# Attention with a soft-capped score, then a soft mixture of experts: a second set of VectorE work buffers and a new table of places

## The chip, the cores and the metric

The kernel runs on one core of one Trainium2 chip, as one program. The metric is the device time of one execution in microseconds (us). The core has a matrix engine (TensorE, PE in the profile; its weight loads are PEld), VectorE (DVE), ScalarE (ACT), GpSimd (POOL) and an engine that here only issues transfers (SyncE, SP). Each engine works through its own instructions in the order in which they were written, and waits on semaphores for the others.

## The reference

```python
# 8 batches, 12 heads, 448 positions, head size 64; cap = 30
scores = cap * np.tanh(scale * (q @ k.T) / cap)
attn   = np.exp(scores - scores.max(-1))             # divided by its sum over the row
x      = (attn / attn.sum(-1)) @ v                   # -> 3584 tokens x 768
logits = x @ phi                                     # 32 slots: 8 experts x 4
d      = softmax(logits, axis=0)                     # over all tokens
slot_input = d.T @ x                                 # 32 x 768
slot_out[e] = np.maximum(slot_input[e] @ w1[e], 0) @ w2[e]   # 768 -> 1024 -> 768
out    = softmax(logits, axis=1) @ slot_out          # 3584 x 768
```

So there is a long attention part, whose output is needed whole before the experts can run (the softmax over all tokens), and a short tail: two small matrix layers with large weights, and an output of 11 MB.

## The kernel before, in words

**Tiles, chunks, steps.** A quad is four heads of a batch, a pair two of them; a pair's scores are 7 tiles of 128 x 448, in each of them 64 keys of either head against its 448 queries. All 336 tiles stand in one list, and six of them are a chunk; there are 56 chunks, and the main loop (L893) has one step j for each. In step j PE makes scores of the next chunk (`qk_chunk`), ACT takes the tanh of chunk j out of PSUM (`tanh_chunk`, L366, two instructions of three tiles, 128x1344) and the exponential of chunk j-1 in SBUF (`exp_chunk`, L374), and PE multiplies the exponentials of a finished pair with v (`pv_first`, `pv_rest`, L627). DVE divides by the row sum (`norm`, L634 and L637).

**Joined tanhs.** For chunks in the tuple `JOINED` the tanh is one instruction over all six tiles (L362, 128x2688). From the first to the last of them the scores have one buffer of six banks, the board, whose halves are written and read in turn; after a joined tanh the scores of the next chunk can begin only when it has ended.

**Shared chunks.** ACT doesn't take all exponentials. In the chunks of the table `SHARED`, DVE computes those of the first one, two or three tiles itself, by seven instructions on the bits of the numbers (`poly_exp`, L596 to L611): four on a tile and constants (tensor_scalar: L602, L604, L606, L609) and three on two tiles (tensor_tensor: L605, L607, L608). They work in place in `ex` and in two work buffers, `xf` and `xp`; the second entry in `SHARED` numbers the set of work buffers, and before there is one set. The exponential of ACT in such a chunk is shorter by those tiles. The table `POLY` says where each of the seven is written: at step j and slot (`'0'`, `'m'`, `'e'`, `'a'` to `'d'`, with `<` and `>` for before and after the other work of a slot).

**Other work in the steps.** `WHEN` says where the rest stands: loads of q and k (on POOL's queue, L185), their transposes by PE with a copy by DVE (`transp`, L281), the transposes of x (`x_transp`, L689), and after each batch its logits, their exponentials E (`e_exp`), the sums over tokens (`slot_sums`, L778), the transposed E (`e_transp`, L733) and their sums (`e_sums`, L743). Before, the table is the same for every batch, shifted by 7 steps. `FILL` and a few single lines write matrix multiplications of ones (`fill`, L657, into unused columns of the pv bank; `spare`, L876) whose results nobody reads.

**The tail** (from L930) ends the last pairs, sums, and runs the two layers (`layer1` L1070, `layer2` L1098). The first layer's weights and part of the second layer's are in SBUF by then; of the second layer's 32 parts (`w2_parts`, 384 KB each) the first `KEPT` are held in SBUF as `w2b`, and the others were cast into DRAM (`w2d`) and are fetched by SP into memory that the attention gives back (`w2t`, L1049). Then 28 output tiles of 128 tokens are multiplied, scaled by ACT and DVE in turn (L1140, L1142 for half tiles, L1193, L1195), and stored by SP (L1126). The last two batches' E are transposed there, between output tiles, by `e_transp`, and their sums are formed by `e_recips` (L748, L751).

The order on every engine is the order in which the program is written (`manual_schedule`); nothing moves an instruction afterwards.

Of the kernel before, what the change touches and what calls it, by code (L numbers as in the profile page):

```python
# [37 lines left out]
def kernel(  # L38
# [28 lines left out]
    KEPT = 11  # L67
# [19 lines left out]
    ET4 = consts.tile([P, B // 2 - 1, NT, 2, HP], BF16, name="ET4")  # L87
# [7 lines left out]
    consts.tile([P, 336], BF16, name="pad")  # L95
# [46 lines left out]
    xf = [wk.tile([P, 3 * S], U16, name="xf")]  # L142
    xp = [wk.tile([P, 3 * S], F16, name="xp")]
# [232 lines left out]
    def exp_chunk(j):  # L376
# [4 lines left out]
    JOINED = (10, 14, 17, 21, 24, 28, 29, 31, 35, 38, 42, 45, 49)  # L381
    SHARED = {1: (2, 0), 3: (3, 0), 4: (3, 0), 6: (2, 0), 7: (3, 0), 9: (3, 0), 11: (3, 0), 12: (3, 0), 14: (3, 0), 16: (3, 0), 18: (3, 0), 19: (3, 0), 21: (3, 0), 23: (3, 0), 25: (3, 0), 26: (3, 0), 28: (3, 0), 30: (3, 0), 32: (3, 0), 33: (3, 0), 35: (3, 0), 37: (3, 0), 39: (3, 0), 40: (3, 0), 42: (3, 0), 44: (3, 0), 46: (3, 0), 47: (2, 0), 48: (2, 0), 49: (3, 0), 51: (2, 0), 52: (1, 0), 53: (3, 0), 54: (1, 0)}
    POLY = {(1, 'm'): ((1, 0),),
            (1, 'e'): ((1, 1),),
            (1, '>a'): ((1, 2),),
            (1, '>b'): ((1, 3),),
            (1, '>d'): ((1, 4),),
            (2, 'r'): ((1, 5),),
            (3, 'e'): ((3, 0),),
            (3, '<a'): ((3, 1), (1, 6)),  # L390
            (3, '<b'): ((3, 2),),
            (3, '>c'): ((3, 3),),
            (4, '<a'): ((3, 4),),
            (4, '>a'): ((3, 5),),
            (4, '<c'): ((4, 0),),
            (5, 'e'): ((4, 1), (3, 6)),
            (5, '<a'): ((4, 2),),
            (5, '>b'): ((4, 3),),
            (5, '>c'): ((4, 4),),
            (6, 'e'): ((6, 0), (4, 5), (6, 1)),  # L400
            (6, '<a'): ((4, 6),),
            (6, '>d'): ((6, 2),),
            (7, 'm'): ((6, 3),),
            (7, 'e'): ((7, 0),),
            (7, '>a'): ((6, 4),),
            (7, '<b'): ((6, 5),),
            (7, '<d'): ((7, 1),),
            (8, '0'): ((7, 2), (7, 3)),
            (8, '>b'): ((6, 6), (7, 4)),
            (8, '>c'): ((7, 5),),  # L410
            (9, 'm'): ((9, 0),),
            (9, '<a'): ((7, 6),),
            (9, '>b'): ((9, 1),),
            (9, '>d'): ((9, 2),),
            (10, 'e'): ((9, 3),),
            (10, '>b'): ((9, 4),),
            (10, '>d'): ((9, 5),),
            (11, 'e'): ((11, 0),),
            (11, '<a'): ((9, 6),),
            (11, '>a'): ((11, 1),),  # L420
            (11, '>b'): ((11, 2),),
            (11, '<c'): ((11, 3),),
            (11, '>c'): ((11, 4),),
            (12, '<a'): ((12, 0),),
            (12, '<b'): ((11, 5),),
            (12, '<c'): ((12, 1),),
            (12, '>d'): ((11, 6),),
            (13, '<b'): ((12, 2),),
            (13, '>b'): ((12, 3),),
            (13, '>c'): ((12, 4),),  # L430
            (13, '>d'): ((12, 5),),
            (14, '<a'): ((14, 0), (12, 6), (14, 1)),
            (14, '<d'): ((14, 2), (14, 3)),
            (15, '>a'): ((14, 4),),
            (15, '>d'): ((14, 5),),
            (16, 'm'): ((14, 6),),
            (16, 'e'): ((16, 0),),
            (16, '<b'): ((16, 1),),
            (16, '>d'): ((16, 2),),
            (17, 'm'): ((16, 3),),  # L440
            (17, '<a'): ((16, 4),),
# [415 lines left out]
    for n in range(2):  # L857
        at(0, "c", vcast, 0, n)
# [376 lines left out]
```

## Time and profile before

| | |
|---|---|
| time, median of 3 runs | 281.52 us (280.67 to 281.65) |
| span of the profiled execution, first to last instruction | 279.2 us |
| busy: ACT, PE, DVE, POOL | 248.6, 247.0, 239.1, 142.0 us |
| granted TensorE clock, mean | 0.985 |
| tanh of three tiles (L366, 128x1344) | 85 times, 1.418 us |
| joined tanh (L362) | 13 times, 2.586 us |
| exponentials on ACT (L374) | 58 times, 110.7 us in all |
| output and weight traffic by SP | 32.02 MB |

The time is taken from outside, around the whole execution; the span lies inside of it, and the difference is what starts and ends a program. The busy time of an engine counts a moment once, also where one instruction begins before the one ahead of it has ended. In the view of groups, "x" is the number of instructions and the number behind the comma the mean duration of one in ns; in the view of time, the first column is the start and the second the duration in us, and what stands in brackets is the idle time of the engine before it and the engine that ended it.

### The profile page before, as it was taken

Reading aid. Unit: us, or ns where it says so; the run is one execution under the profiler, and the core shown is the slowest. Engines: PE = TensorE matmul, PEld = TensorE weight load, DVE = VectorE, ACT = ScalarE, POOL = GpSimd, SP = SyncE. Lnnn points to the kernel's source line nnn. Section 1 sums busy time; section 2 is a strip of 40 time slices with the busy share of each in tenths; the row PEclk is TensorE's granted clock in tenths of the full one; section 3 lists DMA queues with packets and bytes.
Section 4 is the critical chain, followed back from the end, with each engine's and each line's share of the span. In section 5 each row is a group of like instructions: output and inputs, shape, how many; then the busy total and the mean of one; then the engine's idle time right before and its main releaser. Section 6 shows DMA issues by size and latency. Waiting matters only on the chain.

```text
span 279.2 us, 10421 instructions
## 1 busy us (share of the span) xinstructions
PE 247.0 (88%) x4560; PEld 166.6 (60%) x4560; DVE 239.1 (86%) x473; ACT 248.6 (89%) x195; POOL 142.0 (51%) x198
## 2 busy tenths in 40 slices
PE   8898989998999999989999999899999999998720
PEld 7555556756675766566756675657566678553300
DVE  3479999999999999999999999999999997347940
ACT  4999999999999999999999999999999998237720
POOL 8796548662957296728673758375743230200000
PEclk9999999999999999999999999999999999999995
DMA  6999999999999999999999999999999588979997
GB/s 197 277 193 202 219 219 234 229 221 219 224 225 220 219 229 226 225 217 229 223 226 212 213 219 231 218 210 215 231 217 215 117 279 293 367 290 383 434 424 312
DMA packets 57340, 68.08 MB, mean 244 GB/s; under 512 B 4048, under 2 KB 53840, under 8 KB 56784
## 3 DMA queue, kind: packets, MB, share of 16 engines
q0 software_dynamic: 42448, 35.31, 80.0%
q1 hardware_dynamic: 14704, 32.02, 32.6%
q8 instruction: 35, 0.57, 0.7%
q10 hardware_dynamic: 144, 0.10, 0.1%
q14 instruction: 9, 0.07, 0.1%
HBM read 91.72 MB, written 19.27 MB: 398 GB/s over the span
## 4 chain that ended last, share of the span: by engine, by line
ACT 38%; DVE 27%; PE 27%; issue 3%; POOL 1%; ACTq 0%; DVEq 0%
ACT ex L366 15%; ACT ex L374 15%; PE pv L627 8%; ACT ex L362 6%; DVE xq L637 4%; PE sc L349 3%; DVE xp L605 3%; DVE xp L607 3%; DVE ex L608 2%; DVE ex L602 2%; PE so_ps L1098 2%; PE hp L1070 2%; DVE xf L604 2%; DVE ex L609 2%; DVE xp L606 2%
## 5 line engine op out<-in xcount | busy, mean ns | idle before, releaser
L366 ACT ACTIVATE ex<-sc 128x1344 f16<-128x1344 f32 (+1 forms) x87 | 112.9, 1402 | 0.9 <-PE sc L349 0.9
L374 ACT ACTIVATE ex<-ex 128x1344 bf16<-128x1344 f16 (+5 forms) x58 | 110.7, 1916 | 0.1
L627 PE MATMUL pv<-vbd,ex 128*128 128x130 bf16 (+1 forms) x1610 | 94.0, 212 | 7.6 <-POOL vbd L289 3.4
L627 PEld LDWEIGHTS <-ex 128*128 128x128 bf16 (+1 forms) x1680 | 75.6, 101 | 34.9 <-issue 6.2
L289 POOL CAST vbd<-vraw 64x896 bf16<-64x896 f32 x46 | 47.3, 1028 | 57.3 <-PE pv L627 35.7
L349 PE MATMUL sc<-qT,kT 64*64 64x448 bf16 x672 | 66.0, 359 | 6.7 <-ACT ex L366 4.8
L362 ACT ACTIVATE ex<-sc 128x2688 f16<-128x2688 f32 x13 | 33.6, 2586 | 0.0
L349 PEld LDWEIGHTS <-kT 64*64 64x64 bf16 x672 | 22.1, 105 | 16.3 <-ACT ex L366 6.9
L637 DVE TENSOR_TENSOR xq<-pv,rec 128x448 bf16<-128x448 f32 x46 | 28.7, 625 | 1.6
L607 DVE TENSOR_TENSOR xp<-xp,xf 128x1344 f16<-128x1344 f16 (+2 forms) x34 | 27.1, 798 | 0.6
L608 DVE TENSOR_TENSOR ex<-ex,xp 128x1344 uint16<-128x1344 uint16 (+2 forms) x34 | 26.9, 791 | 0.2
L605 DVE TENSOR_TENSOR xp<-xf 128x1344 f16<-128x1344 uint16 (+2 forms) x34 | 26.8, 789 | 0.2
L116 POOL DMA_DIRECT2D w1b<-in_moe_w_dram x32 | 26.3, 825 | 0.0
L602 DVE TENSOR_SCALAR ex<-ex 128x1344 uint16<-128x1344 f16 (+2 forms) x34 | 17.0, 500 | 1.4 <-ACT ex L366 0.8
L606 DVE TENSOR_SCALAR xp<-xp 128x1344 f16<-128x1344 f16 (+2 forms) x34 | 17.2, 505 | 0.6
L281 DVE COPY kT<-kps 128x896 bf16<-128x896 bf16 x23 | 14.2, 617 | 4.0 <-PE kps L276 2.8
L297 POOL MEMSET vbd<- 64x1 bf16 x22 | 2.8, 129 | 28.6 <-PE pv L627 28.3
L604 DVE TENSOR_SCALAR xf<-ex 128x1344 uint16<-128x1344 uint16 (+2 forms) x34 | 16.7, 491 | 0.4
L185 POOL DMA_DIRECT2D qb<-in_q_dram x22 | 16.3, 740 | 1.2 <-PE qps L279 0.5
L609 DVE TENSOR_SCALAR ex<-ex 128x1344 uint16<-128x1344 uint16 (+2 forms) x34 | 16.4, 483 | 0.4
L120 POOL DMA_DIRECT2D w2d<-in_moe_w_dram x21 | 16.4, 816 | 0.0
L185 POOL DMA_DIRECT2D kb<-in_k_dram x22 | 16.3, 739 | 0.0
(124 smaller groups left out, 320.2 us busy)
## 6 DMA issues: line engine op xcount, KB each, us to landing
w1b<-in_moe_w_dram POOLq DMA_DIRECT2D x32, 384.0 KB, 10.2
vraw<-in_v_dram SPq DMA_DIRECT2D x44, 224.0 KB, 6.2
w2d<-in_moe_w_dram POOLq DMA_DIRECT2D x21, 384.0 KB, 9.9
w2t<-w2d SPq DMA_DIRECT2D x21, 384.0 KB, 6.2
qb<-in_q_dram POOLq DMA_DIRECT2D x22, 224.0 KB, 8.2
kb<-in_k_dram POOLq DMA_DIRECT2D x22, 224.0 KB, 8.1
w2b<-in_moe_w_dram POOLq DMA_DIRECT2D x11, 384.0 KB, 9.5
out_dram<-ob SPq DMA_DIRECT2D x2, 1536.0 KB, 7.7
```

Of the source, the lines that this page charges most:

```text
L116: pool.dma_start(out=w1b[e][:, js, fs], in_=w1r[:, e, js, fs])
L185: pool.dma_start(out=t, in_=quad_ap(nm, Q))
L289: pool.tensor_copy(vbds[Q % 2][r, :, :, c0:c0 + DH], raw[r])
L349: ins = pe.matmul(sc[cs, u, 0:S], qkT["k", Q][r, c, cs], qkT["q", Q][r, :, cs], start=True, stop=True).ins
L362: apart["t", i - 1] = apart["t", i] = act.activation(exs[j].bitcast(F16), own["board"][:, :, 0:S], ACT.Tanh, scale=qk_scale / cap).ins
L366: ins = act.activation(exs[j][:, half * CS + u0:half * CS + u1, :].bitcast(F16), (own[0] if i == u0 == 0 else sc)[:, u0:u1, 0:S], ACT.Tanh ...
L374: act.activation(exs[j][:, u0:u1, :], exs[j][:, u0:u1, :].bitcast(F16), ACT.Exp, scale=cap)
L605: lambda: dve.tensor_tensor(p, s, s.bitcast(F16), op=ALU.mult),
L607: lambda: dve.tensor_tensor(p, p, s, op=ALU.mult),
L608: lambda: dve.tensor_tensor(y, y, p, op=ALU.add),
L627: pe.matmul(out_, exs[j][r, u, q0:q0 + (HP if tail else P)], v_, start=(c == 0 and g == gs[0] < NF), stop=(c == NT - 1), skip_group_check= ...
L637: dve.tensor_tensor(xq[Q][:, h, s0:s1, :], pv[:, 0:s1 - s0, 0:DH], rec.to_broadcast([P, s1 - s0, DH]), op=ALU.mult)
```

## The change

- `xf` and `xp` have two copies each (2 x 5.25 KB in each partition), and `SHARED` says for each chunk which set it uses. `SHARED` has 44 chunks for 34: 18 with three tiles, 15 with two and 11 with one, 95 tiles in all; before 27, 5 and 2, 93 tiles. With the new places in `POLY`, the seven instructions of two chunks can stand between one another.
- `JOINED` has 18 chunks for 13, from 7 to 53 for 10 to 49; four times two of them are neighbours (7 and 8, 22 and 23, 35 and 36, 52 and 53), before once (28 and 29).
- `WHEN` is written out for every batch and quad; `FILLS` lists eleven places with `fill` or `spare`; `fill` multiplications go from 262 to 33.
- The E of batches 4 and 5 are kept in buffers of their own and transposed in the tail with those of 6 and 7: `e_recips` and `e_transp` of batch 4 stand ahead of output tile 11, of batch 5 ahead of tile 12, and `e_transp` of the last two ahead of tiles 15 and 17 (before: 13 and 15). `ET4` holds two pairs of batches for three, `ETl` two for one.
- `KEPT` is 10 for 11: one part more of the second layer's weights goes by DRAM (22 for 21).

```diff
-    KEPT = 11
+    EARLY = 4
+    KEPT = 10
...
-    ET4 = consts.tile([P, B // 2 - 1, NT, 2, HP], BF16, name="ET4")
+    ET4 = consts.tile([P, EARLY // 2, NT, 2, HP], BF16, name="ET4")
...
-    xf = [wk.tile([P, 3 * S], U16, name="xf")]
-    xp = [wk.tile([P, 3 * S], F16, name="xp")]
+    xf = [wk.tile([P, 3 * S], U16, name=f"xf{n}") for n in range(2)]
+    xp = [wk.tile([P, 3 * S], F16, name=f"xp{n}") for n in range(2)]
...
-    JOINED = (10, 14, 17, 21, 24, 28, 29, 31, 35, 38, 42, 45, 49)
+    JOINED = (7, 8, 15, 17, 22, 23, 26, 31, 33, 35, 36, 38, 42, 45, 47, 49, 52, 53)
...
-            (55, '0'): ((54, 2),),
-            (55, 'e'): ((54, 3),),
-            (55, '<a'): ((54, 4),),
-            (55, '>a'): ((54, 5), (54, 6))}
+            (55, 'm'): ((53, 5),),
+            (55, 'e'): ((54, 3), (53, 6), (54, 4), (54, 5)),
+            (55, '>a'): ((54, 6),)}
...
     def e_exp(b):
-        es[b] = consts.tile([P, NG, NS], BF16, name="E", tag="E", bufs=2)
+        es[b] = consts.tile([P, NG, NS], BF16, name="E", tag="E", bufs=2) if b < EARLY or b >= B - 2 \
+            else consts.tile([P, NG, NS], BF16, name=f"E{b}")
...
+    def et_home(bb):
+        return ET4[:, bb] if bb < EARLY // 2 else ETl[:, bb - EARLY // 2]
...
-    FILL = ((7, 'a', fill, 25), (6, 'c', spare, 3), (5, 'a', fill, 10), (6, 'd', spare, 6),)
+    FILLS = ((15, '0', spare, 19), (7, '0', spare, 3), (12, 'd', spare, 3), (37, '0', spare, 9), (44, '0', spare, 7), (54, 'd', spare, 34), (33, 'b', fill, 3), (49, 'a', fill, 23), (7, '0', spare, 1), (35, 'a', fill, 7), (46, '0', spare, 1),)
...
-        if n == NH + 3:
-            e_transp(B - 1)
-        if n == NH + 5:
-            e_transp(B - 2)
+        for b, at_n in ((EARLY, NH + 1), (EARLY + 1, NH + 2), (B - 1, NH + 5), (B - 2, NH + 7)):
+            if n == at_n:
+                if b < B - 2:
+                    e_recips(b)
+                e_transp(b)
```

The end of the main loop on DVE, before: the rows from the last batch's sum of slots to the `norm` of the pair that ends in chunk 53. `ex_5289` is chunk 53's buffer (three tiles), `ex_5394` chunk 54's (one tile), `xT` is a copy of transposed x.

```order
L634 RECIPROCAL rec_5456<-pv_5399 128x7
L637 TENSOR_TENSOR xq_5398<-pv_5399,rec_5456 128x448
L689 COPY xT_5461<-xps_5462 128x896
L609 TENSOR_SCALAR ex_5289<-ex_5289 128x1344
L605 TENSOR_TENSOR xp_155<-xf_154 128x448
L606 TENSOR_SCALAR xp_155<-xp_155 128x448
L607 TENSOR_TENSOR xp_155<-xp_155,xf_154 128x448
L689 COPY xT_5504<-xps_5505 128x448
L608 TENSOR_TENSOR ex_5394<-ex_5394,xp_155 128x448
L609 TENSOR_SCALAR ex_5394<-ex_5394 128x448
L634 RECIPROCAL rec_5537<-pv_5490 128x7
L637 TENSOR_TENSOR xq_5398<-pv_5490,rec_5537 128x448
```

The same place on DVE now: between the same two `norm`s. `ex_5066` is chunk 53's buffer (three tiles, set 0), `ex_5171` chunk 54's (two tiles, set 1).

```order
L687 TENSOR_TENSOR xq_5176<-pv_5177,rec_5236 128x448
L657 TENSOR_TENSOR xp0_157<-xp0_157,xf0_155 128x1344
L655 TENSOR_TENSOR xp1_158<-xf1_156 128x896
L658 TENSOR_TENSOR ex_5066<-ex_5066,xp0_157 128x1344
L656 TENSOR_SCALAR xp1_158<-xp1_158 128x896
L659 TENSOR_SCALAR ex_5066<-ex_5066 128x1344
L657 TENSOR_TENSOR xp1_158<-xp1_158,xf1_156 128x896
L658 TENSOR_TENSOR ex_5171<-ex_5171,xp1_158 128x896
L739 COPY xT_5287<-xps_5288 128x448
L659 TENSOR_SCALAR ex_5171<-ex_5171 128x896
L684 RECIPROCAL rec_5319<-pv_5274 128x7
L687 TENSOR_TENSOR xq_5176<-pv_5274,rec_5319 128x448
```

Eight instructions of the polynomials stand between the two `norm`s, three of them over three tiles and five over two; before it was six, one over three tiles and five over one. Chunk 53, on which the next product with v waits, now ends in the middle of this piece.

The output tiles on DVE, before, from tile 11 on. `op` is a product in PSUM, `ob` the buffer for the stores, `eps` transposed E in PSUM.

```order
L1193 TENSOR_SCALAR ob_6179<-op_6181,winv_79 128x768
L733 COPY ETl_5797<-eps_6191 128x7x64
L1193 TENSOR_SCALAR ob_6189<-op_6197,winv_79 128x768
L733 COPY ETl_5797<-eps_6207 128x7x64
L1193 TENSOR_SCALAR ob_6205<-op_6213,winv_79 128x768
L1193 TENSOR_SCALAR ob_6205<-op_6221,winv_79 128x768
```

And now, for the same tiles:

```order
L802 TENSOR_REDUCE zdiag_86<-E4_3776 128x4
L805 RECIPROCAL winv_79<-zdiag_86 64x4
L805 RECIPROCAL winv_79<-zdiag_86 64x3
L787 COPY ETl_5581<-eps_5968 128x7x64
L1260 TENSOR_SCALAR ob_5963<-op_5986,winv_79 128x768
L802 TENSOR_REDUCE zdiag_86<-E5_4417 128x4
L805 RECIPROCAL winv_79<-zdiag_86 64x4
L805 RECIPROCAL winv_79<-zdiag_86 64x3
L787 COPY ETl_5581<-eps_5994 128x7x64
L1260 TENSOR_SCALAR ob_6015<-op_6017,winv_79 128x768
L787 COPY ETl_5581<-eps_6027 128x7x64
L1260 TENSOR_SCALAR ob_6025<-op_6033,winv_79 128x768
```

Eight instructions have come in ahead of tiles 11 and 13, and the copies that stood ahead of 13 and 15 stand ahead of 15 and 17.

More of the change, by code (lines that the diff above doesn't have):

```diff
@@ new lines @@
+            (21, '>b'): ((21, 1),),
+            (22, 'm'): ((21, 2),),
+            (22, 'e'): ((21, 3),),
+            (22, '<b'): ((21, 4),),
+            (22, '>b'): ((21, 5),),
+            (22, '<c'): ((22, 0),),
+            (22, '<d'): ((21, 6),),
+            (23, '0'): ((22, 1),),
+            (23, '>a'): ((22, 2),),
+            (23, '<b'): ((22, 3),),
+            (23, 'r'): ((22, 4),),
+            (23, '>c'): ((22, 5),),
+            (23, '<d'): ((22, 6),),
+            (24, '>a'): ((24, 0),),
@@ L855 @@
         at(j, slot, spare, n, parts)
-    at(34, "<b", fill, 7)
     for n in range(2):
         at(0, "c", vcast, 0, n)
+    for j, slot, f, n in FILLS:
+        at(j, slot, f, n)
     def run(j, slot):
@@ L1053 @@
     pool.memset(hpad, 0.0)
[L1054 removed]
+    ETl = tl.tile([P, (B - EARLY) // 2, NT, 2, HP], BF16, name="ETl")
     def w2_half(n, half):
```

442 lines of the change are left out of this document (235 added, 207 removed), and 25 rows, old and new, of the table WHEN.

## The prediction

> **What bounds the kernel now.** I read the page's busy times first, then the busy times by stage, then what DVE and ACT wait for, and last DVE's instructions one by one.
>
> ```profile
> span 279.2 us, 10421 instructions
> PE 247.0 (88%) x4560; PEld 166.6 (60%) x4560; DVE 239.1 (86%) x473; ACT 248.6 (89%) x195; POOL 142.0 (51%) x198
> ```
>
> The shares mix a main loop and a tail with other limits, so I cut at step 10 (46.3) and at the end of step 55 on DVE (233.4). Columns: stage, length, then busy time of PE, PEld, DVE, ACT, POOL, the granted clock, the DMA engines' share and GB/s.
>
> ```profile
> 12.10:46.30 34.20, 30.18 (x511) 18.79 (x508) 31.00 (x60) 34.16 (x26) 23.52 (x30) 1.00 1.21 207
> 46.30:233.40 187.10, 175.00 (x3490) 123.00 (x3485) 180.75 (x356) 187.10 (x134) 107.43 (x146) 1.00 1.19 221
> ```
>
> ACT is busy 187.10 of 187.10: it is the bound of the loop, and a saving on ACT is worth its whole length as long as nothing else is as long. DVE is the next candidate, with 180.75. What it waits for there:
>
> ```profile
> DVE rec L634 <- PE pv L627: 1.1, 4, 0.3
> DVE ex L602 <- ACT ex L362: 0.5, 2, 0.3
> DVE ex L602 <- ACT ex L366: 0.5, 1, 0.5
> DVE xT L689 <- PE xps L680: 0.3, 1, 0.3
> ```
>
> These waits are 2.4 us together, not the 6.35 that are missing from 187.10. The rest is seen instruction by instruction:
>
> ```profile
> 64.32 0.51 DVE L602 TENSOR_SCALAR ex<-ex 128x1344 uint16<-128x1344 f16 x1
> 64.75 0.50 DVE L609 TENSOR_SCALAR ex<-ex 128x1344 uint16<-128x1344 uint16 x1
> 65.17 0.51 DVE L604 TENSOR_SCALAR xf<-ex 128x1344 uint16<-128x1344 uint16 x1
> 65.58 0.62 DVE L281 COPY qT<-qps 128x896 bf16<-128x896 bf16 x1
> ...
> 67.78 0.51 DVE L606 TENSOR_SCALAR xp<-xp 128x1344 f16<-128x1344 f16 x1
> 68.32 0.86 DVE L607 TENSOR_TENSOR xp<-xp,xf 128x1344 f16<-128x1344 f16 x1
> ```
>
> L609 doesn't read what L602 wrote and begins 0.43 us after it, 0.08 before its end. L607 reads what L606 wrote and begins 0.54 after it, 0.03 after its end. So an instruction costs its duration less 0.08, and 0.11 more if the next one reads its result. The order counts 110 such pairs in the loop; at 0.03 to 0.04 each they are the other 4 us. DVE's room in this stage is therefore 2.4 us, and the stage has two engines that are nearly full.
>
> **The change part by part.**
>
> *ACT.* In the chain of waits:
>
> ```profile
> 54.84 2.36 ACT ex L366 x2
> 57.20 1.21 ACT ex L374
> ...
> 61.99 2.30 ACT ex L362
> 64.29 2.33 ACT ex L374
> ```
>
> Three tiles of exponentials are 2.33 - 1.21 = 1.12 us, one 0.37; two more tiles leave ACT: -0.75. A joined tanh is 2.30 for 2.36; five more: -0.30. There is one exponential per chunk as before. ACT's work falls by 1.05 us, and were it the bound, the loop would fall with it.
>
> *DVE, the polynomials.* Of the seven instructions four have durations like L602, three like L605:
>
> ```profile
> L602 DVE TENSOR_SCALAR ex<-ex 128x1344 uint16<-128x1344 f16 x27 | 14.1, 521 | 1.4 <-ACT ex L366 0.8 <-ACT ex L362 0.5
> L605 DVE TENSOR_TENSOR xp<-xf 128x1344 f16<-128x1344 uint16 x27 | 23.0, 851 | 0.1
> L602 DVE TENSOR_SCALAR ex<-ex 128x448 uint16<-128x448 f16 x2 | 0.5, 270 | 0.0
> L605 DVE TENSOR_TENSOR xp<-xf 128x448 f16<-128x448 uint16 x2 | 0.8, 389 | 0.0
> ```
>
> Three tiles: 4 x 0.521 + 3 x 0.851 = 4.64 us; one: 4 x 0.270 + 3 x 0.389 = 2.25; two, between them: 3.44 (the five measured chunks of two tiles lie a little higher, with transfers of POOL beside them). Before: 27 x 4.64 + 5 x 3.44 + 2 x 2.25 = 147.0. After: 18 x 4.64 + 15 x 3.44 + 11 x 2.25 = 159.9. That is 12.9 more, less the overlap of 70 added instructions, 70 x 0.085 = 6.0: +6.9 us. Two more tiles are a third of it, ten more rounds of seven instructions the rest. The second set of buffers could pay this back by breaking up dependent pairs at 0.11 each, but the order of the changed kernel again has 110 of them: 0.
>
> [...]
>
> *DVE, what leaves the loop.* Two copies of transposed E and one reciprocal:
>
> ```profile
> L733 DVE COPY ET<-eps 128x448 bf16<-128x448 bf16 x6 | 2.3, 380 | 0.0
> L743 DVE RECIPROCAL winv<-wps 128x7 f32<-128x7 f32 x3 | 0.6, 200 | 0.0
> ```
>
> 2 x 0.30 + 0.12 = 0.7 with the overlap taken off. DVE's work in the loop grows by 6.2 us. In steps 0 to 9 the instructions of both orders, at these prices, sum to the same within 0.2 us, so all of it falls behind 46.3, where there is room for 2.4. The other way to meet it is that DVE enters step 10 earlier; by the sums for steps 8 and 9 (less in 8, more in 9) I give that between 0 and 1.3 us, and take 0.8, since the polynomial of chunk 9 still has to wait for its tanh. Steps 53 to 55 are the fullest: DVE has 13.8 us of work there and had 10.9, while ACT has 11.1 and had 12.3. PE waits with `pv_first` for chunk 53's seventh instruction, which now stands in the middle of this piece, and DVE's last `norm` waits for PE's answer; I add 0.3 as a new wait, with bounds of 0 and 0.8, the longest wait that DVE has hereabouts.
>
> *Where DVE's end meets the tail.* The `norm` that ends step 55, the copy behind it, and PE's next step that reads the norm:
>
> ```profile
> 232.74 0.62 DVE L637 TENSOR_TENSOR xq<-pv,rec 128x448 bf16<-128x448 f32 x1
> 234.15 0.39 DVE L689 COPY xT<-xps 128x448 bf16<-128x448 bf16 x1 [0.79 <-PE xps L680]
> ```
> ```profile
> 233.62 0.33 PE L675 MATMUL xps<-ident,xq 128*128 128x128 bf16 x3
> ```
>
> xq is ready at 233.36 and PE takes it at 233.62; from there to the first layer PE goes on without a break worth naming, so whatever DVE is late beyond 0.26 moves the tail. Lateness: 6.2 - 2.4 - 0.8 + 0.3 = 3.3; less 0.26: +3.0 us. ACT's 1.05 us don't count then: ACT waits for scores that stand behind PE's waits for DVE.
>
> *PE.* 229 `fill` multiplications go (mean 188 ns each, overlapping; 9.6 us busy in all):
>
> ```profile
> L657 PE MATMUL pv<-ones 128*128 128x57 bf16 x262 | 9.6, 188 | 0.0
> ```
>
> They cover idle time of an engine with 12.1 us free (187.10 - 175.00): 0, as long as the clock stays at 1.00. The 34 `spare` of step 54 (a dozen multiplications of 384 columns) stand where PE waits for chunk 53: 0; if it doesn't wait there, up to 2 us. Joined tanhs in a row cost ACT a wait only if PE can't fill the board during one exponential; 28 and 29 did it before behind an exponential of six tiles, 22/23 and 52/53 have four tiles (1.58 us): between 0 and 0.3 each, hidden where ACT isn't the bound.
>
> *The tail.* The 22nd part:
>
> ```profile
> w2t<-w2d SPq DMA_DIRECT2D x21, 384.0 KB, 6.2
> ```
> ```profile
> 240.00:248.50 8.50, 8.50 (x208) 5.25 (x200) 4.12 (x15) 1.88 (x4) 1.26 (x1) 1.00 1.01 398
> 248.50:251.00 2.50, 2.50 (x38) 0.70 (x30) 1.21 (x2) 1.61 (x3) 0.00 (x0) 1.00 0.26 101
> 251.00:277.30 26.30, 13.29 (x92) 5.75 (x90) 14.80 (x21) 12.46 (x17) 0.00 (x0) 0.88 1.03 416
> ```
>
> At 398 GB/s it is 1.0 us more of weights, and between the weights and the stores the queues have 2.5 us nearly free: 0 (bounds 0 and 1.0). From 251 on the stores fill the DMA engines at 416 GB/s with PE, ACT and DVE half idle, so the end is their bytes. The moved transposes put two copies and two `e_recips` on DVE ahead of output tiles 11 and 13. The latter's rows:
>
> ```profile
> L748 DVE TENSOR_REDUCE zdiag<-E 128x4 f32<-128x128 bf16 x2 | 0.6, 283 | 0.0
> L751 DVE RECIPROCAL winv<-zdiag 64x4 f32<-64x4 f32 x2 | 0.3, 172 | 0.1
> ```
>
> ```profile
> 260.48 1.97 DVE L1193 TENSOR_SCALAR ob<-op,winv 128x768 f32<-128x768 f32 x2
> ```
>
> 0.32 + 0.19 + 0.12 + 0.30 is 0.93 each, 1.9 in both. The last row ends tile 17 at 262.5, and the store of tiles 14 to 17 goes out with it. The 14 tiles ahead are 14 x 0.393 = 5.5 MB, of which 11.5 us at 416 GB/s have moved 4.8: a backlog of 0.7 MB, 1.7 us. That covers all but 0.2: +0.2, bounds 0 and 1.9.
>
> *Sum.* +3.0 + 0.2 = +3.2 us. The profiled execution has a span of 279.2; the sum makes it 282.4. The runs' median is 281.52, 2.3 above that span, with work that the change doesn't touch: 284.7.
>
> **The rivals.**
>
> 1. *ACT stays the bound* (the other side). DVE may run late without ACT noticing as long as PE has the next scores in time. If the added rounds meet POOL's transfers less often, the loop follows ACT: -1.05, up to -1.7 with ACT's few short waits gone: 279.8 to 280.5, 280.2. It decides if DVE's work grows by less than 2.4 + 0.8 us; the sum says 6.2. For it: ACT has no idle time at all in the stage, so the lateness that DVE has now is hidden, and single instructions of DVE are far from the mean, one beside a transfer's descriptors on POOL:
>
> ```profile
> 152.85 0.92 DVE L606 TENSOR_SCALAR xp<-xp 128x1344 f16<-128x1344 f16 x1
> ```
> ```profile
> 152.01 1.43 POOL L120 DMA_DIRECT2D w2d<-in_moe_w_dram  x2
> ```
>
> It took 0.92 for the 0.51 above. Chance 0.26.
> 2. *PE and the board bind.* Eighteen joined tanhs, each followed by a short exponential: if each of the five new ones costs ACT 0.3 us, ACT's gain is gone and 281.5 to 282.3 comes out, DVE keeping up only by these waits. Against it: PE loses 229 multiplications. Chance 0.06.
> 3. *The tail comes on top.* The stores starve for the 1.9 us and the 22nd part for 1.0: 287. It decides once DVE's work ahead of tile 13 exceeds the backlog. Chance 0.09.
> 4. *The clock falls.* With `fill` gone PE may sit idle long enough in the seven steps without a pair for the granted clock, 1.00 through the loop, to halve for a while. Two us of multiplications in each would take four: up to 14, most of it in PE's free 12.1; I price it +3 on the forecast, 287.5. [...] PE's longest wait of the kind that leads its list is 0.7 us:
>
> ```profile
> PE sc L349 <- ACT ex L366: 3.4, 6, 0.7
> ```
>
> That is far from such a window, and the trace has shown no drop: 0.03.
>
> **How the numbers follow.** Forecast: DVE becomes the bound, 284.7, chance 0.56; its own range is 282.6 (all earlier start, no new wait) to 286.6. Half of the first rival lies more than 0.5% (1.4 us, about what a measurement of this kernel can tell from no change) below 281.52, half within it. Faster: 0.13. Same: 0.13 from rival 1, 0.06 from rival 2, 0.05 from the low end of the forecast: 0.24. Slower: 0.51 + 0.09 + 0.03 = 0.63. The range that leaves out no more than 2 in 10 runs from 280.1 (half of rival 1 outside) to 287.0.
>
> **What would show it.** In the profile after: DVE busy in the loop with hardly any wait, ACT with idle time whose releaser is PE's sc, PE with waits on DVE's ex and xq (L659, L687); the same 110 dependent pairs; the `norm` before the x transposes some 3 us later against the start; the stage of stores as long as before. If ACT is busy without a gap and DVE still waits 2 us or more in the loop, the forecast is wrong at its main term, the price of the added rounds; if the loop ends as forecast but the whole doesn't, the tail is.

## The result

The changed kernel takes 294.79 us (median of 4 runs, 293.07 to 296.58), the kernel before 281.14 beside it: a ratio of 1.0485, 95% interval 1.043 to 1.054. The forecast was 284.7, range 280.1 to 287.0: the direction is right, the size is not. One run of `e1` and one of `e16` below, over 1.5% above the fastest of their kernel, are left out of their times. The profiled executions, 279.2 and 294.8 us long, part at these places (times from the span's start):

| | before | after | later by |
|---|---|---|---|
| first tanh begins | 6.14 | 6.90 | 0.76 |
| last tanh ends | 232.89 | 241.41 | 8.5 |
| last `norm` of the loop ends (L637, now L687) | 233.36 | 245.13 | 11.8 |
| first half output tile begins | 249.38 | 261.89 | 12.5 |
| last transfer lands | 277.82 | 293.08 | 15.3 |

The first line isn't the change's: it lies between 5.8 and 7.0 in the runs below, whatever the kernel.

### The profile page after: what moved, and what is told of

It reads as the page before. It is cut to its first block, busy times and chain, and to the rows that moved or that the text cites. A ratio compares the mean times of both kernels' runs of the same rounds, so it can differ in the third digit from the quotient of the medians.

```text
span 294.8 us, 10051 instructions
## 1 busy us (share of the span) xinstructions
PE 247.7 (84%) x4332; PEld 165.2 (56%) x4332; DVE 250.8 (85%) x548; ACT 249.3 (85%) x190; POOL 138.0 (47%) x198
## 4 chain that ended last, share of the span: by engine, by line
DVE 52%; PE 33%; ACT 6%; issue 2%; DMA 1%; POOL 1%; POOLq 0%; ACTq 0%
PE pv L677 10%; DVE xq L687 7%; DVE xp L655 6%; DVE ex L658 6%; DVE xp L657 6%; DVE xp L656 4%; PE sc L350 4%; DVE xf L654 4%; DVE ex L652 3%; ACT ex L367 3%; DVE ex L659 3%; DVE xT L739 3%; DVE kT L282 3%; DVE qT L282 3%; PE junk L942 2%
## 5 line engine op out<-in xcount | busy, mean ns | idle before, releaser
L677 PE MATMUL pv<-vbd,ex 128*128 128x130 bf16 (+1 forms) x1610 | 96.9, 216 | 10.8 <-DVE ex L659 4.3
L375 ACT ACTIVATE ex<-ex 128x1344 bf16<-128x1344 f16 (+5 forms) x58 | 102.6, 1774 | 0.1
L367 ACT ACTIVATE ex<-sc 128x1344 f16<-128x1344 f32 (+1 forms) x77 | 95.5, 1290 | 4.7 <-PE sc L350 4.4
L677 PEld LDWEIGHTS <-ex 128*128 128x128 bf16 (+1 forms) x1680 | 78.8, 103 | 36.5 <-issue 8.0
L363 ACT ACTIVATE ex<-sc 128x2688 f16<-128x2688 f32 x18 | 43.5, 2417 | 3.5 <-PE sc L350 3.4
L687 DVE TENSOR_TENSOR xq<-pv,rec 128x448 bf16<-128x448 f32 x46 | 28.7, 624 | 1.5
L658 DVE TENSOR_TENSOR ex<-ex,xp 128x1344 uint16<-128x1344 uint16 (+2 forms) x44 | 29.7, 678 | 0.2
L655 DVE TENSOR_TENSOR xp<-xf 128x1344 f16<-128x1344 uint16 (+2 forms) x44 | 29.1, 663 | 0.4
L656 DVE TENSOR_SCALAR xp<-xp 128x1344 f16<-128x1344 f16 (+2 forms) x44 | 19.6, 449 | 0.7
L654 DVE TENSOR_SCALAR xf<-ex 128x1344 uint16<-128x1344 uint16 (+2 forms) x44 | 19.1, 435 | 0.4
L659 DVE TENSOR_SCALAR ex<-ex 128x1344 uint16<-128x1344 uint16 (+2 forms) x44 | 19.3, 438 | 0.2
L298 POOL MEMSET vbd<- 64x1 bf16 x22 | 3.0, 137 | 31.6 <-PE pv L677 31.4
```

What stands on the lines that cost most here:

```text
L363: apart["t", i - 1] = apart["t", i] = act.activation(exs[j].bitcast(F16), own["board"][:, :, 0:S], ACT.Tanh, scale=qk_scale / cap).ins
L367: ins = act.activation(exs[j][:, half * CS + u0:half * CS + u1, :].bitcast(F16), (own[0] if i == u0 == 0 else sc)[:, u0:u1, 0:S], ACT.Tanh ...
L375: act.activation(exs[j][:, u0:u1, :], exs[j][:, u0:u1, :].bitcast(F16), ACT.Exp, scale=cap)
L655: lambda: dve.tensor_tensor(p, s, s.bitcast(F16), op=ALU.mult),
L658: lambda: dve.tensor_tensor(y, y, p, op=ALU.add),
L677: pe.matmul(out_, exs[j][r, u, q0:q0 + (HP if tail else P)], v_, start=(c == 0 and g == gs[0] < NF), stop=(c == NT - 1), skip_group_check= ...
```

## The profile after

The page's busy times and the row of the granted clock (40 slices; 9 is 90% or more):

```profile
span 294.8 us, 10051 instructions
PE 247.7 (84%) x4332; PEld 165.2 (56%) x4332; DVE 250.8 (85%) x548; ACT 249.3 (85%) x190; POOL 138.0 (47%) x198
...
PEclk9999899988999799959999999999999999999975
```

The row of the clock before:

```profile
PEclk9999999999999999999999999999999999999995
```

ACT and PE work as long as before, within 0.7 us, DVE 11.7 us longer. New are four places, 30.7 us apart, where the clock falls. (This execution is the slowest of the four, 296.58 us with a mean clock of 0.951; the three others had 0.956 to 0.967, so their clock fell for less time.) By windows, a place that precedes a fall and the place itself (columns as in the prediction):

```profile
30.60:34.00 3.40, 1.27 (x20) 0.43 (x20) 3.33 (x8) 3.40 (x4) 1.97 (x3) 1.00 1.20 238
34.00:37.40 3.40, 3.29 (x40) 2.38 (x36) 3.05 (x7) 3.40 (x3) 0.00 (x0) 0.50 1.23 228
...
122.80:126.20 3.40, 1.55 (x29) 0.86 (x23) 3.33 (x8) 3.40 (x4) 1.65 (x3) 1.00 1.24 197
126.20:133.00 6.80, 6.44 (x71) 4.12 (x72) 5.55 (x15) 5.49 (x5) 2.42 (x4) 0.50 1.17 193
```

The clock is at 0.50 for 3.4, 3.4, 3.4 and 6.8 us, 17.1 together, each time behind a window in which PE worked for 37% to 61% of the time (the two not shown: 1.84 of 3.40, 2.12 of 3.50). How this comes about and what it costs, at the last of them, from the view of time:

```profile
125.58 0.62 DVE L658 TENSOR_TENSOR ex<-ex,xp 128x896 uint16<-128x896 uint16 x1
126.12 0.39 DVE L659 TENSOR_SCALAR ex<-ex 128x896 uint16<-128x896 uint16 x1
```
```profile
123.77 0.69 PE L677 MATMUL pv<-vbd,ex 128*128 128x130 bf16 x9
126.56 0.70 PE L677 MATMUL pv<-vbd,ex 128*128 128x130 bf16 x5 [2.10 <-DVE ex L659]
```
```profile
128.59 1.35 ACT L367 ACTIVATE ex<-sc 128x1344 f16<-128x1344 f32 x1
131.24 1.29 ACT L367 ACTIVATE ex<-sc 128x1344 f16<-128x1344 f32 x1 [1.31 <-PE sc L350]
```

PE waits 2.10 us for the last instruction of a polynomial, then works at half clock, and 5 us later ACT, which had no idle time in the 18 us before, waits 1.31 us for scores. ACT's waits in the loop:

```profile
ACT ex L363 <- PE sc L350: 3.4, 5, 1.1
ACT ex L367 <- PE sc L350: 2.7, 4, 1.3
```

The end of the loop on DVE, ACT and PE:

```profile
242.29 0.62 DVE L657 TENSOR_TENSOR xp<-xp,xf 128x896 f16<-128x896 f16 x1
242.95 0.62 DVE L658 TENSOR_TENSOR ex<-ex,xp 128x896 uint16<-128x896 uint16 x1
243.49 0.38 DVE L739 COPY xT<-xps 128x448 bf16<-128x448 bf16 x1
243.79 0.38 DVE L659 TENSOR_SCALAR ex<-ex 128x896 uint16<-128x896 uint16 x1
244.26 0.21 DVE L684 RECIPROCAL rec<-pv 128x7 f32<-128x7 f32 x1
244.50 0.62 DVE L687 TENSOR_TENSOR xq<-pv,rec 128x448 bf16<-128x448 f32 x1
```
```profile
240.08 1.33 ACT L367 ACTIVATE ex<-sc 128x1344 f16<-128x1344 f32 x1
```

DVE ends 3.7 us behind the last tanh (before 0.5), and from 235.7 it has no wait above 0.1 us.

## The experiments

Differences are to the kernel before, measured beside each (281.1 to 281.5). The three last columns are of the one profiled execution: "halved" is the time at half clock up to the last tanh; "DVE's work" adds up its instructions to the last `norm`: durations, less overlaps, plus gaps of up to 0.06 us; "waits" are the longer gaps.

| run | time | difference | halved | DVE's work | waits |
|---|---|---|---|---|---|
| before | 281.2 | | 0 | 219.9 | 12.6 |
| after | 294.79 | +13.7 | 17.1 | 229.9 | 14.4 |
| `e1_fill_back` | 299.04 | +17.9 | 6.8 | 229.9 | 16.8 |
| `e2_fill_gone` | 288.38 | +7.2 | 3.4 | 221.5 | 15.5 |
| `e5_tables_alone` | 312.77 | +31.6 | 17.1 | 235.3 | 23.4 |
| `e6_four_fills` | 295.16 | +14.0 | 13.7 | 229.3 | 15.3 |
| `e7_short_poly` | 291.72 | +10.5 | 17.1 | 220.8 | 18.5 |
| `e4_no_small_chunks` | 296.51 | +15.3 | 13.7 | 216.2 | 26.9 |
| `e9_dve_work_in_before` | 286.78 | +5.5 | 0 | 227.7 | 9.8 |
| `e8_no_step54_spares` | 298.02 | +16.8 | 17.1 | 229.0 | 15.0 |
| `e10_fill_in_gaps` | 289.47 | +8.2 | 0 | 228.5 | 9.4 |
| `e11_short_end` | 293.00 | +11.7 | 10.2 | 226.3 | 13.1 |
| `e3b_tail_back` | 299.09 | +17.8 | 17.1 | 229.9 | 16.5 |
| `e12_all_three` | 295.03 | +13.7 | 10.2 | 227.8 | 14.9 |
| `e13_gaps_and_end` | 288.83 | +7.4 | 3.4 | 225.7 | 12.0 |
| `e14_two_parts_more` | 283.54 | +2.1 | 3.4 | 221.5 | 12.4 |
| `e15_gaps_short_poly` | 286.46 | +5.0 | 0 | 221.2 | 14.5 |
| `e16_three_gaps` | 289.95 | +8.5 | 0 | 228.2 | 9.8 |
| `e17_gaps_end_step9` | 290.43 | +9.1 | 3.4 | 226.5 | 11.6 |
| `e18_first_gap` | 290.67 | +9.3 | 3.4 | 228.7 | 10.3 |

**The fills, and the tables by themselves.**

`e1` is the changed kernel with the `FILL` of before; `e2` the reverse, in the kernel before; `e6` adds to the changed kernel; `e5` puts `JOINED`, `SHARED`, `POLY` and the two sets of buffers into the kernel before, with two parts of weights fewer in SBUF to make room. The main lines of e1 and e6, and of e5 the one that isn't in the change:

```diff
-    FILLS = ((15, '0', spare, 19), (7, '0', spare, 3), (12, 'd', spare, 3), (37, '0', spare, 9), (44, '0', spare, 7), (54, 'd', spare, 34), (33, 'b', fill, 3), (49, 'a', fill, 23), (7, '0', spare, 1), (35, 'a', fill, 7), (46, '0', spare, 1),)
+    FILL = ((7, 'a', fill, 25), (6, 'c', spare, 3), (5, 'a', fill, 10), (6, 'd', spare, 6),)
```
```diff
+    for j in (7, 14, 21, 28):
+        at(j, "a", fill, 25)
```
```diff
-    KEPT = 11
+    KEPT = 9
```

> The changed kernel with the places of `fill` and `spare` of the kernel before (FILL in every batch, 7 `fill` at step 34) instead of the list FILLS; nothing else. Theory A (the clock): the four half-clock stretches of the changed kernel come from the 229 `fill` multiplications that went, and they make most of the 11.8 us by which its loop is longer; with the multiplications back the granted clock is 1.00 through the loop, ACT's 8 us of waits for scores in the loop shrink to 3 or less, and the time falls by 6 to 9 us to 286 to 289. Theory B (DVE alone): the added rounds of the polynomials make the loop 11.8 us longer by themselves and the low clock is a consequence that lies in PE's free time: 293.5 to 295.5, whatever the clock does.

> The kernel before with the list FILLS of the changed kernel in the place of its own `fill` and `spare`; nothing else. Theory A: the windows of the steps without a pair now have PE busy for less than about 0.6 of 3.4 us, the clock halves in two to six of them, and as ACT is without a gap here, every score that comes late counts: 284 to 291. Theory B: 281 to 282, clock 1.00 or not. A third way (C): the clock fell in the changed kernel only because its PE waits for DVE, so that here nothing falls: clock 1.00 and 281 to 282.

> The changed kernel with 25 `fill` added at slot 'a' of steps 7, 14, 21 and 28 alone (100 multiplications of 57 columns, some 0.7 us of PE in each place). Theory A: the share of busy PE in the four windows rises by 0.2 from 0.38, 0.54, 0.61 and 0.47; the drops that stood at 0.54 and 0.61 go for certain, the others perhaps; each drop that goes gives back 1.5 to 2.5 us: 286 to 291. Theory B: no change, 294 to 295.5.

> The kernel before with JOINED, SHARED, POLY and the two sets of work buffers of the changed kernel; its own WHEN, FILL and tail, but 9 parts of the second layer's weights kept in SBUF for 11 (the room for the second set). If the forecast's sum for DVE holds: DVE's end 3 us later, clock 1.00, tail 0 to 2 us for two parts more: 284 to 287. If DVE's added work is hidden (ACT stays the bound): 280 to 283. If the tables alone are worth the whole loss: 292 to 295. That these polynomials stand beside another WHEN can cost or save a microsecond.

No theory came through. e1 and e5 lie outside of what any expected, e6 is theory B's, and e2 lies in theory A's range, but not by A's way. The old places of `fill` made the changed kernel slower, though the clock fell in fewer places (two in the loop, a third at 245 us, where the 34 `spare` of step 54 are missing); why is not shown. In the kernel before, the new list cost 7.2 us with one fall only in its profiled execution: the last tanh came 1.8 us later, the last `norm` another 2.6 (there PE goes through the 34 `spare` where it hadn't waited), the rest in the tail, 1.7 of it between the first layer and the first half tile, where PE waited 1.2 us with no releaser, and 1.5 in the stores. The 100 multiplications of e6 missed the gaps: the clock still fell four times. And the tables without their `WHEN` cost 32 us: the places of polynomials and of transposes were chosen together and can't be judged apart.

**DVE's work.**

`e7`, which leaves out the last columns of DVE's exponentials, and `e8` edit the changed kernel, and `e4` takes the eleven chunks with one tile out of its two tables; `e9` edits the kernel before (`padt` is an unused tile of 336 columns). The lines of e7, e9 and e8:

```diff
-        n1 = tiles * S
+        n1 = tiles * 408
```
```diff
+    for j in range(8, 56, 2):
+        at(j, "c", lambda: dve.tensor_tensor(padt, padt, padt, op=ALU.mult))
```
```diff
-(54, 'd', spare, 34),
```

> The changed kernel with each of the polynomials' instructions shortened to 408 of 448 columns of a tile, so that a part of the exponentials isn't computed; the order, the number of instructions and the waits stay. By the durations in the changed kernel's trace this takes some 9.9 us off DVE's work up to its last norm, which is what that work grew by (219.9 to 229.9). Theory D (DVE's throughput: its work is 9.9 us more, not 6.2, and there is no room for any of it): the loop falls by 8 to 12 us, time 283 to 287. Theory P (the places: waits that the new order makes among PE, DVE and ACT, whatever an instruction takes): it falls by at most 4 us, 290.5 or more.

> The changed kernel with its eleven chunks of one shared tile taken out of SHARED and POLY: 33 chunks and 84 tiles; everything is computed, ACT takes the eleven tiles. DVE's work falls by 11 x 2.40 - 77 x 0.085 = 19.9 us, ACT's grows by 11 x 0.37 = 4.1. Theory D: DVE is no longer the bound, ACT is, at some 3 us above its loop in the kernel before, with the longer tail on top: 284 to 289. Theory P, or ACT as the bound: the waits stay and ACT's work comes on top, 294 to 299.

> The kernel before with 24 multiplications of 128x336 on DVE that nobody reads, one in every second step from 8 to 54: at some 0.33 us less 0.085 they add 5.9 us to DVE's work, nothing else. The prediction's room (2.4 us of waits, nothing else changed): 281.2 + 3.3 = 284 to 285. No room at all (theory D, as the changed kernel's waits suggest, which didn't shrink): 286.5 to 287.5. If DVE's lateness stays hidden behind ACT: 281 to 282.

> The changed kernel without the 34 `spare` multiplications of step 54. If they stand where PE waits for DVE anyway, as the prediction has it: 294 to 295.5. If they delay PE's last products, as the kernel before with the new list of fills suggests (its DVE ended 3.1 us behind the last tanh, before 0.5): 291.5 to 293.

In the changed kernel DVE's work alone wasn't what held it: 9.1 us less of it gave 3.2 us, and 13.7 us less (e4) nothing, though there ACT takes the eleven tiles, 4.1 us by the expectation's price; the clock fell in both. In the kernel before the added work cost 5.5 us, which by the time alone is the "no room" of the expectation; the trace says otherwise. The added instructions of e9 and a group that nobody edited; the same group in the kernel before; and the stage of the prediction in e9:

```profile
L859 DVE TENSOR_TENSOR pad<-pad 128x336 bf16<-128x336 bf16 x24 | 8.3, 347 | 0.0
...
L607 DVE TENSOR_SCALAR xp<-xp 128x1344 f16<-128x1344 f16 x27 | 15.2, 563 | 0.5
```
```profile
L606 DVE TENSOR_SCALAR xp<-xp 128x1344 f16<-128x1344 f16 x27 | 14.6, 540 | 0.5
```
```profile
46.30:233.40 187.10, 170.30 (x3410) 120.94 (x3411) 183.08 (x365) 183.71 (x130) 106.59 (x146) 1.00 1.18 213
```

The 24 were meant as 5.9 us; DVE's work rose by 7.7, since the three-tile tensor_scalars got longer too, 563 for 540 ns in this group. Its waits fell by 2.8, and the last `norm` came 4.9 later. So the trace agrees with the room in the prediction (2.4), and the price of the added work was too low: 7.7 us for 5.9.

The `spare` of step 54 hold the clock up. The end of the loop on PE without them (e8), and the same product in the changed kernel:

```profile
241.30 0.51 PE L677 MATMUL pv<-vbd,ex 128*128 128x130 bf16 x3 [1.72 <-DVE ex L659]
...
243.86 2.46 PE L677 MATMUL pvm<-vbd,ex 128*128 128x130 bf16 x21
```
```profile
244.15 1.37 PE L677 MATMUL pvm<-vbd,ex 128*128 128x130 bf16 x21
```

Without them PE waits idle for DVE, the clock is halved at 241.0 (in the changed kernel it is 1.00 from 239 to 246), and the product takes 2.46 us for 1.37. All four executions of e8 had a mean clock of 0.941 or 0.942.

**Fill in the gaps, the end, the tail.**

All four edit the changed kernel: `e10` and `e11` (which also takes chunk 54 out of `SHARED` and `POLY`) the list `FILLS`, `e3b` the two numbers and the places that go with them, `e12` all of these:

```diff
+(5, 'c', fill, 20), (6, 'a', fill, 45), (12, 'd', fill, 45), (20, 'c', fill, 15), (20, 'd', fill, 15), (28, 'e', fill, 40),
```
```diff
-(54, 'd', spare, 34),
+(54, 'd', spare, 10),
```
```diff
-    EARLY = 4
-    KEPT = 10
+    EARLY = 6
+    KEPT = 9
```

> The changed kernel with 180 more `fill` multiplications (27 ns each), put where its PE stood idle in or just before the windows that the four half-clock stretches follow: 20 and 45 ahead of the scores of steps 5 and 6, 45 at the end of step 12, 15 and 15 in step 20, 40 ahead of step 28's product with v; nothing else. In the changed kernel's trace ACT's waits that come 2 to 6 us after the start of a half-clock stretch are 0.81, 1.14 and 0.81, 0.82, 1.31: 4.9 us. Theory C (the halved clock costs what follows it): with the four stretches gone 290 to 291.5. If PE is late for DVE alone, and the low clock lies in time that is lost anyway: 294 to 295.5, the clock at 1.00 or not.

> The changed kernel with chunk 54 (two tiles) out of SHARED and 10 `spare` for 34 in step 54: everything is computed. DVE loses 4 x 0.39 + 3 x 0.62 - 7 x 0.085 = 2.8 us in steps 54 and 55, PE 1.6 us ahead of the last products, ACT gets 0.75 us more. In the changed kernel DVE works without a wait from 235.7 to 244.2 and its last norm ends 3.7 us behind the last tanh (before 0.5). If this piece is what makes the end late: the norm some 2 to 2.7 us earlier against the start, 292 to 293. If the end only follows what came before: 294.5 to 296.

> The changed kernel with the transposed E of batches 4 and 5 formed in the loop as in the kernel before (steps 41 and 48, their sums at step 50), the two others ahead of output tiles 13 and 15, and 9 parts of the second layer's weights kept for 10 (the room for it). In the trace of the changed kernel the stage from the first to the last whole output tile took 12.27 us, before 10.59. If the moved transposes cost that: this stage back at 10.6 and the tail behind the last norm 1 to 2 us shorter than 49.7, less what one part more of weights costs (up to 1.0), while the loop gets 0.9 us of DVE's work: 293 to 295. If the stores' bytes set the end: no change or 1 us more, 294.5 to 296.

> The edits of the three kernels beside it together. If the halved clock, the end of step 55 and the tail are separate and each is worth what its own run is to show (4, 2.3 and 0.8 us): 286 to 288.5. If they hide one another: 290 or more.

e10 tells what the clock is worth. In its profiled execution the row of the clock, its loop to the last `norm`, and the window that answers to 30.60:34.00 are:

```profile
PEclk9999999999999999999999999999999999999985
```
```profile
46.30:238.75 192.45, 173.01 (x3385) 120.85 (x3386) 187.63 (x417) 188.76 (x132) 106.16 (x146) 1.00 1.17 215
...
30.00:33.40 3.40, 2.98 (x80) 2.15 (x78) 3.33 (x7) 3.40 (x3) 1.68 (x3) 1.00 1.21 234
```

180 multiplications more, and the kernel is 5.5 us faster (8.2 us above the kernel before for 13.7), a ratio of 1.0295 to the kernel before (1.0266 to 1.0324). ACT's waits behind the first tanh fall from 7.1 us to 2.7 (one of 1.0, at 71.3, is there without a fall too), DVE's from 14.4 to 9.4. The 180 only add work to PE, so what they gave back is the clock's. The last `norm` is still 5.4 us later than before and 3.7 behind the last tanh.

e11 gave 1.9 us, but with another pattern of the clock; its `norm` ends 1.85 us behind the tanh. e3b put the two copies and the sums back into the loop, which got 2.2 us longer, though by waits: DVE's work is the same 229.9. The whole output tiles took 10.58 us again (changed kernel 12.27, before 10.59), yet the stores then ended 11.6 us behind the last tile, where before it was 9.6. e12 had its clock fall at two other places, so its time tells nothing of the three edits; but its tail, without the moved transposes, is as long as e13's with them (48.4 us from the last `norm` to the end in both).

**What is left of 8.2 us.** `e13` is e10 with the edit of e11, `e15` e10 with that of e7, `e16` e10 without its last entry, `e18` the changed kernel with e10's first two entries, `e17` is e13 with one entry more; `e14` is the kernel before with `KEPT = 9`:

```diff
+(9, '<b', fill, 30),
```

> The changed kernel with the 180 `fill` in PE's gaps and with the shorter end (chunk 54 out of SHARED, 10 `spare` for 34 in step 54) together. With the clock at 1.00 the changed kernel took 289.5 us and its last norm ended 3.7 us behind the last tanh; with the shorter end alone that was 1.85. If this piece is on the path: 287 to 288.5. If it is not, since PE or ACT end as late by other work: 289 to 290.5.

> The kernel before with 9 parts of the second layer's weights kept in SBUF for 11, so that 23 for 21 are fetched in the tail; nothing else. If a part is hidden by the 2.5 us in which the queues are nearly free (the prediction's price of 0): 281 to 282. If the bytes set the tail's end: 2 x 1.0 us, 282.8 to 283.8.

> The changed kernel with the 180 `fill` in PE's gaps, and the polynomials cut to 408 of 448 columns (some 10 us of DVE's work gone, a part of the exponentials not computed). With the clock falling, that cut was worth 3.1 us. If DVE is the bound of the changed kernel once the clock stays at 1.00, as the forecast had it: 284 to 287, 3 us or more below 289.5. If DVE's work is not what remains: 288 to 289.5.

> The changed kernel with the `fill` in PE's gaps but without the 40 ahead of step 28's product with v. If each stretch has its own cause in the window ahead of it: the first three stretches are gone, the one at some 126 us from the start is back, ACT has its wait of 1.3 us behind it, and the time lies 1 to 2 us above 289.5. If one drop brings the next: clock 1.00 throughout, 289 to 290.

> The changed kernel with `fill` in PE's gaps, the shorter end, and 30 more `fill` at step 9 ahead of the x transposes, where PE stood idle for 1.04 us ahead of the one half-clock stretch (45 to 49 us from the start) that the run without these 30 had. If that stretch cost it about 1 us, as a stretch cost the changed kernel (5.3 us for five windows of 3.4), the end is worth some 1.6 us and shows now: 287.3 to 288.2, clock 1.00 through the loop. If the end is hidden behind other work: 288.5 to 289.5.

> The changed kernel with the first group of `fill` alone: 20 and 45 ahead of the scores of steps 5 and 6. The run without the fourth group had no stretch left at all, against what was expected. If the first stretch brings the others on (its lateness makes the later gaps): clock 1.00, 289.5 to 290.5. If each has its own gap: the three others stay, 292.5 to 294.

DVE first. With the clock up, e15's cut (7.3 us of DVE's work against e10) gives 3.2 us, and ACT is the bound again:

```profile
46.30:233.40 187.10, 170.22 (x3338) 117.61 (x3329) 178.53 (x412) 186.77 (x131) 104.24 (x146) 1.00 1.20 220
```

Its last tanh ends 0.26 us later than before after a start that was 0.65 later. The gain is no larger than e7's; what tells the two apart is ACT, whose waits behind the first tanh are 3.8 us in e7 and 0.5 here, so that here it is ACT that stops the gain. So e10's loop is bound by DVE, as the forecast had it. What stays is the end: e15's last `norm` is 3.4 us behind the tanh.

The end by itself isn't settled. e13 and e17 shorten it (1.85 us), but ACT, which takes chunk 54's tiles, and one half-clock stretch each put the last tanh 1.6 and 2.0 us later than in e10; the last `norm` comes within 0.25 us of e10's, and the whole is 0.8 us faster in one run and 0.9 slower in the other.

The clock: the profiled executions of e16 and e18 contradict that each stretch has a cause of its own. Without the fourth group the fourth stretch stayed away, and the first group alone gives 4.4 us and leaves one stretch:

```profile
PEclk9999999999998999999999999999999999999985
```

So most of the later gaps may follow from the first lateness. But these are single executions, and the falls change from one to the next: e16's two others had a mean clock of 0.976 and 0.969 for 0.983 in the profile, e18's 0.960 to 0.974 for 0.977, and two of e10's 0.978 and 0.971 for 0.983 (a fall of 3.4 us takes 0.006 off the mean). Phase may have a part, which no run tried: in the changed kernel the first three stretches last 3.413 us each, and the later falls begin 9, 18 and 27 times that behind the first; and e10 and e13 have the same gap of PE, 1.04 us at 43.4, and only in e13 did the clock fall behind it.

What doesn't hang on single profiles is the price. The changed kernel, e10, e16 and e18 differ in dummy multiplications alone. Of their 15 executions, the ten with a mean clock of 0.969 or more took 288.84 to 290.85 us, the five with 0.967 or less 293.07 to 296.58.

The tail: two parts more of weights in the kernel before (e14, ratio 1.0068, 1.0044 to 1.0091) cost 2.1 us, and how stays open. In the profiled execution it isn't the bytes: from the first layer to the last landing it is as long as before within 0.1 us, and the clock fell at 232 us, where the last products stood. But five other executions had a mean clock of 0.983 to 0.985, like the kernel before, and took 282.75 to 284.63; without a trace of them, the bytes' 2.0 us aren't excluded. What the tail does show is the rate of the stores. Eight microseconds of half-tile stores, with the DMA engines full, in the order: e14, the kernel before, e5 (the same tail code and `KEPT` as e14, but two sets of work buffers and the change's smaller `pad`, see below), the changed kernel:

```profile
254.70:262.70 8.00, 6.91 (x56) 3.10 (x45) 6.85 (x12) 6.03 (x10) 0.00 (x0) 1.00 1.04 386
```
```profile
253.40:261.40 8.00, 6.69 (x36) 3.04 (x35) 7.33 (x12) 6.29 (x10) 0.00 (x0) 1.00 1.05 392
```
```profile
279.60:287.60 8.00, 6.69 (x36) 3.04 (x35) 7.34 (x12) 6.20 (x10) 0.00 (x0) 1.00 1.04 366
```
```profile
265.90:273.90 8.00, 5.81 (x57) 2.50 (x55) 7.24 (x17) 5.18 (x8) 0.00 (x0) 1.00 1.04 365
```

A packet of 1536 bytes takes 65 ns on average in every kernel with one set of work buffers (before, e2, e9, e14) and 69 in every one with two. All packets of the stores together keep each of the 16 DMA engines busy for 27.1 us in the first and 28.0 in the second: 0.9 more. From the first half tile to the last landing it is 28.4 us in e14 and in the kernel before, and 30.1 in e5; but e2 takes 29.9 with packets of 65 ns, since its last packets, of 9216 bytes, land one behind the other, 0.34 us apart. So the length of the stage isn't the packets' alone. The store buffers lie at other places in SBUF: at 63488, 75776 and 100352, multiples of 512, in the first; at 61664, 73952 and 98528, 32 bytes off a multiple of 64, in the changed kernel. It isn't the second set that moves them: in e5 they lie 544 bytes lower than before, and that is what an unused tile, `pad`, gives up, which the diff shrinks from 336 to 64 columns of two bytes and the list of the change leaves out. That the address makes the packets slower fits these runs, but wasn't tried by itself.

## Why the prediction was wrong

- **The clock.** The step that failed is "They cover idle time of an engine with 12.1 us free (187.10 - 175.00): 0, as long as the clock stays at 1.00", with rival 4 at 0.03. It fell, for 17.1 us in the profiled execution, and cost 5.5 (13.7 less e10's 8.2, by medians; the two profiled executions are 7.7 apart). The argument against it, that PE's longest wait of that kind was 0.7 us, came from a trace in which the `fill` still stood and DVE was on time; and that trace's only fall, at 271.0 in the tail, stood behind 3.8 us without any work of PE (267.2 to 271.0). In the changed kernel PE's longest gaps ahead of the four falls were 1.82, 1.40, 0.61 and 2.10 us. The rival's price, +3, was low, and its picture incomplete: the missing `fill` alone brought one fall (e2), the new tables with the old `fill` two in the loop (e1), both together four.
- **What stood ahead of a fall.** No run shows how long PE has to be idle before the clock falls, the window that rival 4 holds its 0.7 us against. What the runs showed in its place: in the changed kernel's loop the clock stayed at 0.50 for 3.41 us or twice that, and PE was not idle all the while before: it was busy for 1.27 of 3.40 us ahead of the first fall and for 2.12 of 3.50 ahead of the third. Which share decides, the runs don't say: a window with less than the 61% stayed without a fall (e1: 54% at 126 us).
- **DVE's main term.** The mechanism is right: with the clock up (e10) the last `norm` came 5.4 us later, where 3.3 was forecast, and e15 shows DVE as the bound. The room was right (2.4 + 0.8 = 3.2; the waits fell by 3.2). Mis-sized is the price of the added rounds, 12.9 less the overlap: DVE's work grew by 8.6 us in e10 for 6.2. The polynomials take 164 to 165 us for the 159.9 of the sum, and 148.1 before for its 147.0: 16 to 17 more for 12.9. Rounds of one, two and three tiles each bring about a third of the 4.5 us by which e10's lie above the sum, and most of it is in the tensor_scalars that met POOL's transfers: in the changed kernel a one-tile tensor_scalar took 268 ns alone and 314 beside a DMA_DIRECT2D on POOL, one of three tiles 503 and 579. The two one-tile chunks of the kernel before had met none, and I took their mean. The last `norm`'s 3.7 us behind the tanh are in this sum; 0.3 was set for the wait at chunk 53. Two figures beside the sum don't follow from its terms: the low end of the forecast's own range, 282.6, would be 283.9 by the bounds given for the start and the wait, and rival 3's 287 would be 287.4.
- **ACT.** By its durations less overlaps, 0.9 of the 1.05 us saved shows in e15, 0.4 in e10, none in the changed kernel (0.6 more); its waits in the loop are for PE's scores, as "What would show it" had it. The 110 dependent pairs at no gain stand: the gaps up to 0.06 us sum to 4.1 us in both.
- **The 34 `spare`.** That they cost nothing where PE waits for chunk 53 holds, and more: without them the kernel is 3.1 us slower.
- **The 22nd part.** 0 from the first layer on in e14's profile, as priced; but e14's two parts cost 2.1 us in the median, which the fall in that profile doesn't explain for the other executions. Up to 1 us of the 13.7 may be this part's.
- **The moved transposes.** The stage of whole output tiles got 1.7 us longer, near the upper bound of 1.9, but the end of the stores doesn't follow it (e3b, e12): +0.2 for them may stand. But the stage of the stores is not as long as before: 31.2 us from the first half tile to the last landing for 28.4. Of the tail's surplus, 2.5 us in e10 and 3.8 in the changed kernel, the slower packets are 0.9; no term of the sum had that. The rest isn't explained.

The loss, split up: 5.5 (clock, from the medians) + 5.4 (last `norm`) + 2.5 (tail), both from the profiles of e10 and of the kernel before, = 13.4 for 13.7. The parts are taken as differences along one line, so that they add up proves nothing; how sure each is stands above.

## What to carry to other kernels

Dummy multiplications held the clock here only where PE was idle in the order that ran: 100 in other places left four falls (e6), 180 in the gaps none in the profiled loop (e10). After a change of order, look for the new gaps, from the first one on, before anything else is judged. Price added instructions from rows that stand in the same company (here beside POOL's transfers, 314 ns for 268), not from the two that happened to stand alone. And a tile that grows or shrinks can move the buffers behind it, an unused tile too (`pad`, 544 bytes): compare the time of a packet before and after (here 65 and 69 ns).

## What was not expected of the hardware

The clock fell behind windows in which PE was busy for up to 61% (71% in e11), with no wait of PE above 2.4 us in the loop of the changed kernel, e1, e2, e4, e5 or e7. Falls of 17.1 us in the profiled execution, fewer in the others, cost 5.5 us in the median although PE had had 12 us free, and behind each ACT waited for scores, 0.8 to 1.3 us, ending 4.6 to 5.5 us after the fall. A store packet of 1536 bytes took 69 ns instead of 65 on average in every kernel whose store buffers had moved.
